# Where 1/sum is applied in windowed attention: on the weights per unit, or on the output per pair

## The chip, the cores and the metric

The kernel runs on one core of a Trainium2 chip. The metric is device time in microseconds, the median of several executions. A core has TensorE (matmuls, and the transpositions that are matmuls with an identity), VectorE, ScalarE, GpSimd, each with one in-order queue of instructions, and SyncE (SP), which issues DMAs. In profiles they are PE (PEld for its weight loads), DVE, ACT, POOL and SP.

## The reference

Attention with a sliding window of 128 and a few sink keys, followed by a dense two-layer block; batch 4, 8 heads, 768 positions, 64 per head, 512 to 2048 to 512 in the dense block:

```python
scores = scale * np.matmul(q, k.transpose(0, 1, 3, 2))
keep = is_sink | in_window
scores = np.where(keep, scores, -1000000000.0)
scores = scores - np.max(scores, axis=-1, keepdims=True)
a = np.exp(scores)
a = a / (np.sum(a, axis=-1, keepdims=True) + 1e-09)
x = np.matmul(a, v)                  # (B, H, S, D), then to (B*S, H*D)
h = x @ w_in
r = np.maximum(h, 0.0)
out = (s * (r * r) + b) @ w_out
```

## The kernel before, in words

**Chunks.** The 3072 rows are worked on in eight chunks of 384 (`ORDER`: batch and half of the sequence). While the dense block of chunk c runs (`moe_steps`: 16 steps `l1`, 16 steps `l2`, the latter two `f` behind), the attention of chunk c + 1 is issued between its steps. The main loop at L775 deals out the attention's slots evenly over the steps, over all but the last two of them. The first two chunks, both with keys of the first half only, use `Plain`, which normalises on VectorE (L523); the change does not touch it. Chunks three to eight use `attn_slots` (L413).

**Numbers as two parts.** A matmul operand in `F32R` holds only part of a float32. Where precision matters a value is split in a high part (a cast on ScalarE) and the rest (a subtraction), and the product is made from several matmuls: 12 of 384 columns per `l1` (L602), 9 of 512 per `l2` (L621).

**Units.** In `attn_slots` a chunk has 24 units: 8 heads times 3 blocks of 128 queries, two heads to a pair, two pairs to a quad. One slot issues the parts of several units:

- `unit_a` (slot t, unit t): the scores of 128 queries against two key blocks of 128 and 8 sink keys (L303, L304), on VectorE mask and minimum (L308), on ScalarE the exponential with its sum (L314). The mask leaves two triangles that don't overlap, so GpSimd adds the two 128-column squares into one (L317); the first unit of a batch has one square only. GpSimd copies the 8 sink exponentials, three times over, into `psk`, a tile per quad (L318).
- `turn` (slot t, unit t - 3): TensorE transposes the added square (L324) into a corner of the bank in which the next unit's scores are made.
- `unit_b` (unit t - 4): VectorE parts the triangles again (L337), ScalarE and GpSimd make the high and low parts `hl` (L339, L340). For the last unit of a pair it also makes 1/sum of the pair's six sums on VectorE (L349 to L353), in two parts, and puts them into columns 96 and up of `psk` (L352 on GpSimd).
- `unit_c` (unit t - 7): the products with the values (L369, L377), at the end of a head the copy to `pp.x` (L384, L385), at the end of a quad three transpositions of `psk` (L392) into `xs`.
- `sinks` (L397) then adds the sinks' product to a pair's `pp.x`, and `scaled` (L404) multiplies `xs` with `sel`, a constant of ones and zeros that gives each column's 1/sum to all rows of a head, multiplies `pp.x` by that on VectorE (L409), and splits the result in the two parts of the dense block's input `k.x` (L410, L411). `LD` and `LDL` give the slots of these two.

`sm`, the unit's exponentials, has four buffers (`SMB`). All short-lived PSUM tiles (`sc`, `o`, `h`, `ts`, `os`, `zb`) share the five banks of `psA`.

**Order.** The source order is a priority. A planner places each engine's instructions by its own model of times, among those that are ready the earliest in the source first; so instructions of neighbouring slots and steps stand mixed. What results is a fixed order per engine; on the chip each waits on semaphores for its inputs and for its buffer.

## Time and profile before

| | |
|---|---|
| median of 3 runs | 734.43 us (733.99 to 736.96) |
| profiled execution | 733.62 us, of which the span of its instructions is 731.8 us |
| TensorE matmuls busy | 697.6 us, 95% of the span |
| VectorE, ScalarE, GpSimd busy | 514.5 us (70%), 473.4 us (65%), 390.7 us (53%) |
| mean granted clock of TensorE | 0.977 |

The dense block of the first chunk starts at about 45 us and settles at about 133, until when weights are loaded and prepared. The windowed attention runs from about 150 to 655 us, beside the dense block of chunks two to seven; the last chunk's dense block has nothing beside it. Busy times of matmuls overlap, so that the time one takes is read from the start of the next. Idle time of an engine is shown with what ended it.

### The profile page before, as it was taken

Reading aid. Unit: us, or ns where it says so; the run is one execution under the profiler, and the core shown is the slowest. Engines: PE = TensorE matmul, PEld = TensorE weight load, DVE = VectorE, ACT = ScalarE, POOL = GpSimd, SP = SyncE. Lnnn points to the kernel's source line nnn. Section 1 sums busy time; section 2 is a strip of 40 time slices with the busy share of each in tenths; the row PEclk is TensorE's granted clock in tenths of the full one; section 3 lists DMA queues with packets and bytes.
Section 4 is the critical chain, followed back from the end, with each engine's and each line's share of the span. In section 5 each row is a group of like instructions: output and inputs, shape, how many; then the busy total and the mean of one; then the engine's idle time right before and its main releaser. Section 6 shows DMA issues by size and latency. Waiting matters only on the chain.

```text
span 731.8 us, 11834 instructions
## 1 busy us (share of the span) xinstructions
PE 697.6 (95%) x3812; PEld 614.7 (84%) x3812; DVE 514.5 (70%) x1202; ACT 473.4 (65%) x1157; POOL 390.7 (53%) x640
## 2 busy tenths in 40 slices
PE   6788889899999999999999999999999999999996
PEld 3367667789988999899998999899999999989895
DVE  6779999748985688757786588847786579743331
ACT  5978887558774687657784677747775577633222
POOL 2254555348983588816674388915765389810000
PEclk8889989999999999999999999999999999999999
DMA  7845122041310221111111222112111212000001
GB/s 277 344 172 194 34 91 83 12 142 42 95 57 16 94 59 55 43 62 53 45 51 56 73 68 66 45 42 61 56 52 56 72 42 63 8 15 30 0 1 47
DMA packets 27221, 52.62 MB, mean 72 GB/s; under 512 B 3472, under 2 KB 15376, under 8 KB 25232
## 3 DMA queue, kind: packets, MB, share of 16 engines
q1 hardware_dynamic: 27152, 51.79, 21.3%
q8 instruction: 32, 0.52, 0.3%
q14 instruction: 37, 0.30, 0.1%
HBM read 45.49 MB, written 6.29 MB: 71 GB/s over the span
## 4 chain that ended last, share of the span: by engine, by line
PE 76%; DVE 11%; POOL 4%; DMA 3%; ACT 3%; issue 2%; SPq 1%; POOLq 0%; ACTq 0%; DVEq 0%
PE po L621 32%; PE h L602 31%; PE o L377 3%; PE sc L303 2%; PE sc L304 2%; PE sc L324 2%; DMA vf<-in_v 2%; DVE w L214 2%; DMA w<-in_w 2%; DVE g L610 1%; DVE wt L213 1%; POOL w L216 1%; PE o L555 1%; DVE smf L532 1%; DVE w L225 1%
## 5 line engine op out<-in xcount | busy, mean ns | idle before, releaser
L602 PE MATMUL h<-x,w 128*128 128x384 f32 x1536 | 297.1, 342 | 3.2 <-DVE y L409 2.0
L621 PE MATMUL po<-w,g 128*128 128x512 f32 x1152 | 297.5, 404 | 0.0
L602 PEld LDWEIGHTS h<-x,w 128*128 128x128 f32 x1536 | 266.5, 189 | 9.7 <-DVE y L409 2.5
L621 PEld LDWEIGHTS po<-w,g 128*128 128x128 f32 x1152 | 211.0, 190 | 45.3 <-issue 2.7
L607 DVE SCALAR_TENSOR_TENSOR r<-h,sb,r 128x384 f32<-128x384 f32 x128 | 78.7, 615 | 83.1 <-ACT r L605 82.2
L610 DVE SCALAR_TENSOR_TENSOR g<-r,sb,g 128x384 fp32r<-128x384 f32 x128 | 109.1, 852 | 34.9 <-ACT g L609 33.3
L605 ACT ACTIVATE r<-h 128x384 f32<-128x384 f32 x128 | 62.4, 488 | 89.2 <-PE h L602 80.8
L340 POOL TENSOR_TENSOR hl<-two,hl 128x256 fp32r<-128x256 f32 x128 | 102.2, 800 | 15.1 <-ACT hl L339 12.9
L609 ACT ACTIVATE g<-r,sb 128x384 fp32r<-128x384 f32 x128 | 78.9, 617 | 33.1 <-DVE r L607 32.2
L317 POOL TENSOR_TENSOR sm<-sm 128x128 f32<-128x128 f32 x128 | 67.4, 527 | 60.1 <-ACT sm L314 56.7
L314 ACT ACTIVATE sm<-sm,negm 128x264 f32<-128x264 f32 (+1 forms) x144 | 72.0, 500 | 28.6 <-DVE negm L308 27.1
L284 POOL TENSOR_TENSOR kl<-kraw,kh 128x528 fp32r<-128x528 f32 (+1 forms) x48 | 60.4, 1258 | 25.9 <-ACT kh L282 25.7
L339 ACT CAST hl<-two 128x256 fp32r<-128x256 f32 x128 | 50.4, 394 | 25.8 <-DVE two L337 25.7
L216 POOL TENSOR_TENSOR w<-w 128x1024 int32<-128x1024 int32 (+1 forms) x17 | 32.6, 1918 | 55.2 <-DVE w L214 34.7
L337 DVE TENSOR_TENSOR two<-sc,split 128x256 f32<-128x256 f32 x128 | 53.1, 417 | 5.8 <-POOL hl L340 5.5
L377 PE MATMUL o<-hl,vv 128*128 128x256 f32 (+1 forms) x256 | 44.3, 275 | 0.0
L318 POOL COPY psk<-sm 128x24 f32<-128x24 f32 x144 | 35.0, 243 | 17.2 <-ACT sm L314 17.0
L283 DVE TENSOR_TENSOR qs<-qraw,qs 64x384 fp32r<-64x384 f32 x48 | 39.7, 827 | 3.8 <-ACT qs L279 2.3
L377 PEld LDWEIGHTS o<-hl,vv 128*128 128x128 f32 x256 | 39.6, 188 | 3.2
L308 DVE CUSTOM_DVE_ANT_0 sm<-sc,msk 128x264 f32<-128x264 f32 (+1 forms) x80 | 32.0, 399 | 14.1 <-PE sc L304 13.5
L303 PE MATMUL sc<-kh,qs 128*128 128x264 f32 (+1 forms) x144 | 41.6, 291 | 0.0
L308 DVE CUSTOM_DVE_ANT_0 sm<-sc,m_all 128x264 f32<-128x264 f32 x64 | 27.3, 426 | 20.3 <-PE sc L304 18.8
(129 smaller groups left out, 916.5 us busy)
## 6 DMA issues: line engine op xcount, KB each, us to landing
w<-in_w SPq DMA_DIRECT2D x15, 1024.0 KB, 9.8
kraw<-in_kT SPq DMA_DIRECT2D x32, 264.0 KB, 2.6
out<-ot SPq DMA_DIRECT2D x24, 256.0 KB, 2.0
qraw<-in_qT SPq DMA_DIRECT2D x24, 192.0 KB, 2.4
vraw<-in_v SPq DMA_DIRECT2D x16, 256.0 KB, 2.7
kraw<-in_kT SPq DMA_DIRECT2D x16, 200.0 KB, 2.4
vsraw<-in_vsk SPq DMA_DIRECT2D x24, 64.0 KB, 2.0
vraw<-in_v SPq DMA_DIRECT2D x8, 192.0 KB, 2.4
```

What stands on the lines that cost most here:

```text
L284: nc.gpsimd.tensor_tensor(out=hd.kl[:, :kw], in0=hd.k[:, :kw], in1=hd.kh[:, :kw].bitcast(F32), op=ALU.subtract)
L308: nc.vector.tensor_tensor_reduce(out=sm[:, :n], in0=sc[:, :n], in1=m, scale=-0.125, scalar=BIG, op0=ALU.add, op1=ALU.min, accum_out=negm[: ...
L314: nc.scalar.activation(sm[:, :n], sm[:, :n], AF.Exp, bias=negm[:, uu], scale=-1.0, accum_out=pp.zz[:, i, hh:hh + 1])
L317: nc.gpsimd.tensor_tensor(out=sm[:, c1:c1 + P], in0=sm[:, p1:p1 + P], in1=sm[:, c1:c1 + P], op=ALU.add)
L340: nc.gpsimd.tensor_tensor(out=lo, in0=both, in1=hi.bitcast(F32), op=ALU.subtract)
L377: nc.tensor.matmul(hd.o[:, q0:q0 + n * P], hd.vv[:, kb, :], hd.hl[:, t, c0 * P:(c0 + n) * P], start=(hd.n == 0), stop=(i == BLK - 1 and kb ...
L602: nc.tensor.matmul(h[:, :CH], weight[f][:, 0, wi, cc * P:(cc + 1) * P], x[xi][:, cc, :], start=(i == 0), stop=(i == 11))
L605: nc.scalar.activation(r, h[:, :CH], AF.Relu, scale=1.0 / WUP)
L607: nc.vector.scalar_tensor_tensor(out=r, in0=h[:, :CH], scalar=sw_ap, in1=r, op0=ALU.mult, op1=ALU.mult)
L609: nc.scalar.activation(gg[:, 0, :], r, AF.Identity, bias=b_ap, scale=1.0)
L610: nc.vector.scalar_tensor_tensor(out=gg[:, 1, :], in0=r, scalar=b_ap, in1=gg[:, 0, :].bitcast(F32), op0=ALU.add, op1=ALU.subtract)
L621: nc.tensor.matmul(po[tb], gg[:, gi, tsl], weight[f][:, 1, wi, :], start=(f == 0 and i == 0), stop=(f == NF - 1 and i == 2))
```

## The change

From the third chunk on (all of `attn_slots`), 1/sum is applied to the weights before the transposition. A new function `norm` runs in every even slot for the two units before: on VectorE it adds 1e-9 to the two sums and takes the reciprocals, on ScalarE it multiplies each unit's added square by its 1/sum, and on GpSimd the sinks' exponentials are multiplied by it on the way into `psk`, in place of the copy. `sel`, the 1/sum columns in `psk`, `scaled` and its product go; `sinks` ends a pair. The slots of `sinks` change (`LD`, `LDL`), and a chunk has 32 slots in place of 33.

```diff
--- before.py
+++ after.py
@@ -34,7 +34,7 @@
 RB, VB = 1, 2
 E0 = 8
 FN, FB, FC = (4, 2), (6, 6), (9, 10)
-LB, LC, LD, LDL, L2 = 4, 7, ((3, 4), (6, 7)), ((2, 2), (3, 3)), 2
+LB, LC, LD, LDL, L2 = 4, 7, (3, 5), (2, 2), 2
 
 
 @with_exitstack
@@ -85,8 +85,6 @@
 
 
 
-    sel = const.tile([P, 2, P], F32R, tag="sel", name="sel")
-
     psks = [const.tile([P, BLK, P], F32, tag=f"psk{i}", name=f"psk{i}") for i in range(2)]
 
     lim = const.tile([P, 2, 2], I32, tag="lim", name="lim")
@@ -132,13 +130,6 @@
 
     def constants2():
 
-        spread = wk.tile([P, 2, P], F32, tag="y", name="spread", bufs=3)
-        nc.gpsimd.memset(spread, 0.0)
-        for j in range(4):
-            row = spread[96:P, j // 2].rearrange("p (a d) -> p a d", a=2)
-            nc.gpsimd.affine_select(out=row, in_=row, pattern=[[1, 2], [0, D]], compare_op=ALU.not_equal, fill=1.0,
-                                    base=2 * j, channel_multiplier=-1)
-        nc.scalar.copy(sel, spread)
         for t in psks:
             nc.gpsimd.memset(t, 0.0)
 
@@ -252,7 +243,7 @@
             hd.q, hd.v = pp.q[hd.half], pp.v[:, :, hh]
             k.heads[2 * pr + hh] = hd
         pp.psk = psks[(k.c * (H // 4) + pr // 2) % 2]
-        pp.zz = wk.tile([P, BLK, 2], F32, tag="zz", name="zz", bufs=2)
+        pp.z = wk.tile([P, 3, 2 * BLK], F32, tag="zz", name="zz", bufs=2)
 
     def load_keys(k, h):
 
@@ -309,14 +300,26 @@
                                        op0=ALU.add, op1=ALU.min, accum_out=negm[:, uu])
 
         k.cc[(h, i)] = (sm,) + ((NS, None, 0) if g == 0 else (P, 0, 2 * P) if g % 2 else (P + NS, 0, P))
-        s0 = k.cc[(h, i)][3]
-        hh = h % 2
-        nc.scalar.activation(sm[:, :n], sm[:, :n], AF.Exp, bias=negm[:, uu], scale=-1.0, accum_out=pp.zz[:, i, hh:hh + 1])
+        nc.scalar.activation(sm[:, :n], sm[:, :n], AF.Exp, bias=negm[:, uu], scale=-1.0,
+                             accum_out=pp.z[:, 0, h % 2 * BLK + i:h % 2 * BLK + i + 1])
         if g > 0:
             c1, p1 = k.cc[(h, i)][1:3]
             nc.gpsimd.tensor_tensor(out=sm[:, c1:c1 + P], in0=sm[:, p1:p1 + P], in1=sm[:, c1:c1 + P], op=ALU.add)
-        nc.gpsimd.tensor_copy(out=pp.psk[:, i, :12 * NS].rearrange("p (t x) -> p t x", t=3)[:, :, h % 4 * NS:(h % 4 + 1) * NS],
-                              in_=sm[:, s0:s0 + NS].unsqueeze(1).to_broadcast([P, 3, NS]))
+
+    def norm(k, *two):
+
+        z = k.pairs[two[0][0] // 2].z
+        j0 = two[0][0] % 2 * BLK + two[0][1]
+        jj = slice(j0, j0 + 2)
+        nc.vector.tensor_scalar(out=z[:, 1, jj], in0=z[:, 0, jj], scalar1=1e-9, scalar2=None, op0=ALU.add)
+        nc.vector.reciprocal(out=z[:, 2, jj], in_=z[:, 1, jj])
+        for j, (h, i) in enumerate(two):
+            pp = k.pairs[h // 2]
+            sm, c0, _, s0 = k.cc[(h, i)]
+            rz = z[:, 2, j0 + j:j0 + j + 1]
+            nc.scalar.mul(sm[:, c0:c0 + P], sm[:, c0:c0 + P], rz)
+            nc.gpsimd.tensor_scalar(out=pp.psk[:, i, :12 * NS].rearrange("p (t x) -> p t x", t=3)[:, :, h % 4 * NS:(h % 4 + 1) * NS],
+                                    in0=sm[:, s0:s0 + NS].unsqueeze(1).to_broadcast([P, 3, NS]), scalar1=rz, scalar2=None, op0=ALU.mult)
 
     def turn(k, h, i, tp):
 
@@ -341,16 +344,6 @@
         else:
             nc.scalar.copy(hi, tp)
             nc.vector.tensor_tensor(out=lo, in0=tp, in1=hi.bitcast(F32), op=ALU.subtract)
-        pp = k.pairs[h // 2]
-        if h % 2 == 1 and i == BLK - 1:
-            z0 = 12 * NS + h // 2 % 2 * 4
-            zr = wk.tile([P, 2, BLK, 2], F32, tag="zr", name="zr")
-            zh = wk.tile([P, BLK, 2], F32R, tag="zh", name="zh")
-            nc.vector.tensor_scalar(out=zr[:, 0], in0=pp.zz, scalar1=1e-9, scalar2=None, op0=ALU.add)
-            nc.vector.reciprocal(out=zr[:, 1], in_=zr[:, 0])
-            nc.vector.tensor_copy(zh, zr[:, 1])
-            nc.gpsimd.tensor_copy(out=pp.psk[:, :, z0:z0 + 2], in_=zh.bitcast(F32))
-            nc.vector.tensor_tensor(out=pp.psk[:, :, z0 + 2:z0 + 4], in0=zr[:, 1], in1=zh.bitcast(F32), op=ALU.subtract)
 
     def unit_c(k, h, i):
 
@@ -400,13 +393,6 @@
         os_ = ps("os")
         nc.tensor.matmul(os_[:, :CH], pp.vs, pp.xs, start=True, stop=True)
         nc.vector.tensor_tensor(out=pp.x, in0=os_[:, :CH], in1=pp.x, op=ALU.add)
-
-    def scaled(k, pr):
-
-        pp = k.pairs[pr]
-        zb = ps("zb")
-        nc.tensor.matmul(zb[:, :CH], sel[:, pr % 2], pp.xs, start=True, stop=True)
-        nc.vector.tensor_tensor(out=pp.x, in0=zb[:, :CH], in1=pp.x, op=ALU.mult)
         nc.scalar.copy(k.x[0][:, pr, :], pp.x)
         (nc.vector if pr == H // 2 - 1 else nc.gpsimd).tensor_tensor(out=k.x[1][:, pr, :], in0=pp.x, in1=k.x[0][:, pr, :].bitcast(F32), op=ALU.subtract)
 
@@ -424,8 +410,7 @@
         ends = {}
         for pr in range(H // 2):
             t = 4 * BLK * (pr // 2 + 1) - 1 + LC
-            for d, fn in zip((LD if pr < H // 2 - 2 else LDL)[pr % 2], (sinks, scaled)):
-                ends.setdefault(t + d, []).append((fn, pr))
+            ends.setdefault(t + (LD if pr < H // 2 - 2 else LDL)[pr % 2], []).append((sinks, pr))
 
         def slot(t):
             def f():
@@ -440,6 +425,8 @@
                     unit_a(k, *units[t], k.bank)
                 if 0 <= t - LB < n:
                     unit_b(k, *units[t - LB], k.bank[:, 3 * P:])
+                if t % 2 == 0 and 0 < t <= n:
+                    norm(k, *units[t - 2:t])
                 for fn, pr in ends.get(t, ()):
                     fn(k, pr)
                 if t + 1 < n + LB:
@@ -448,7 +435,7 @@
                     turn(k, *units[t + 1 - LB], k.bank[:, 3 * P:])
             return f
 
-        parts = [slot(t) for t in range(n + LC + LDL[1][1])]
+        parts = [slot(t) for t in range(n + LC + LDL[1])]
         parts.pop(n + LB)
         return k, parts
 
```

## Rows read from the trace of the kernel before

**Rows 1.** Stretches: us, busy PE, PEld, DVE, ACT, POOL, clock, DMA share, GB/s

```profile
323.00:405.00 82.00, 82.00 (x463) 75.26 (x462) 59.57 (x147) 54.78 (x149) 47.15 (x87) 1.00 0.18 57
405.00:491.00 86.00, 85.53 (x483) 78.29 (x482) 62.68 (x147) 58.52 (x150) 58.15 (x103) 1.00 0.18 56
```

**Rows 2.** Chain of waits, 431 to 448 us: start, length in us, what

```profile
433.32 0.41 PE o L377 x4
...
434.86 2.10 PE po L621 x9
...
440.24 2.10 PE po L621 x9
...
445.47 2.10 PE po L621 x9
```

**Rows 3.** By line and shape: count | busy us, mean ns | idle before

```profile
L602 PE MATMUL h<-x,w 128*128 128x384 f32 x1536 | 297.1, 342 | 3.2 <-DVE y L409 2.0 <-ACT tf L546 1.2
...
L409 DVE TENSOR_TENSOR y<-zb,y 128x384 f32<-128x384 f32 x24 | 13.2, 552 | 0.7
...
L350 DVE RECIPROCAL zr<-zr 128x6 f32<-128x6 f32 x24 | 4.6, 191 | 0.8
...
L351 DVE CAST zh<-zr 128x6 fp32r<-128x6 f32 x24 | 7.7, 322 | 0.5
...
L353 DVE TENSOR_TENSOR psk<-zr,zh 128x6 f32<-128x6 f32 x24 | 7.2, 302 | 0.7
...
L521 ACT ACTIVATE smf<-smf,negm 128x128 f32<-128x128 f32 x8 | 3.1, 389 | 1.9 <-DVE negm L519 1.9
...
L270 ACT CAST vs<-vsraw 128x128 fp32r<-128x128 f32 x24 | 6.6, 295 | 0.8 <-DMA vsraw<-in_vsk 0.8
...
L532 DVE TENSOR_SCALAR sm<-sm,zf 128x128 f32<-128x128 f32 x8 | 1.9, 284 | 0.1
...
L610 DVE SCALAR_TENSOR_TENSOR g<-r,sb,g 128x384 fp32r<-128x384 f32 x128 | 109.1, 852 | 34.9 <-ACT g L609 33.3
...
L609 ACT ACTIVATE g<-r,sb 128x384 fp32r<-128x384 f32 x128 | 78.9, 617 | 33.1 <-DVE r L607 32.2
```

**Rows 4.** List of waits, whole execution: us in total, times, longest us

```profile
PE h L602 <- DVE y L409: 2.0, 3, 1.1
```

**Rows 5.** In order of time, TensorE, 401 us: start, length in us, what

```profile
401.19 0.34 PE L408 MATMUL zb<-xsk,sel 128*128 128x384 f32 x1
401.36 0.40 PE L621 MATMUL po<-w,g 128*128 128x512 f32 x1
```

**Rows 6.** In order of time, 303 to 305 us: VectorE, TensorE

```profile
303.64 0.56 DVE L409 TENSOR_TENSOR y<-zb,y 128x384 f32<-128x384 f32 x1
...
304.26 0.97 PE L602 MATMUL h<-x,w 128*128 128x384 f32 x4 [0.43 <-DVE y L409]
```

**Rows 7.** In order of time, GpSimd, first 8 us

```profile
7.37 0.52 POOL L159 COPY msk<-m_all 128x128 bf16<-128x128 bf16 x2 [3.27 <-DVE m_all L101]
```

**Rows 8.** L349 and L318 alone: ns shortest/median/longest, first and last start

```profile
L349 DVE TENSOR_SCALAR zr<-zz x24: 207/322/803, 167.5 to 633.2; 128x6 f32<-128x6 f32 x24
...
L318 POOL COPY psk<-sm x144: 193/203/546, 156.7 to 634.0; 128x24 f32<-128x24 f32 x144
```

**Rows 9.** In order of time: L314's read, then L324, three pairs

```profile
157.33 0.19 ACT L314 ACTIVATION_READ_ACCUMULATOR sm<-sm,negm 128x1 f32 x1
159.06 0.27 PE L324 MATMUL sc<-identr,sm 128*128 128x128 f32 x1
...
520.97 0.18 ACT L314 ACTIVATION_READ_ACCUMULATOR sm<-sm,negm 128x1 f32 x1
521.66 0.27 PE L324 MATMUL sc<-identr,sm 128*128 128x128 f32 x1
...
632.97 0.19 ACT L314 ACTIVATION_READ_ACCUMULATOR sm<-sm,negm 128x1 f32 x1
635.98 0.27 PE L324 MATMUL sc<-identr,sm 128*128 128x128 f32 x1
```

## The prediction

> **What bounds the kernel now.** I read the busy time by stage first. From 323 to 405 us TensorE's matmuls are busy for 82.00 of 82.00 us, from 405 to 491 for 85.53 of 86, both at a granted clock of 1.00, the 2.4 GHz level [rows 1]. VectorE stands at 59.6 and 62.7, ScalarE at 54.8 and 58.5, GpSimd at 47.2 and 58.2 in the same stretches [rows 1]. A busy TensorE row alone is weak evidence, as matmuls overlap; so I read the chain of waits over 15 us of one chunk [rows 2]: it steps from matmul group to matmul group, with no other engine between. In the six chunks with the windowed attention the time is therefore the sum of what TensorE is given, plus what it waits. Third, the groups by line tell where it waits: before L602 it sat idle 3.2 us in the whole execution, and 2.0 of them ended with VectorE's L409, a line that the change deletes [rows 3]; the list of waits has three of these, the longest of 1.1 us [rows 4]. Fourth, the instructions in order of time around one use of the deleted product and around one of the waits [rows 5, 6].
>
> **What is removed, on the path.** (a) The product with `sel`, L408: 24 matmuls, one per pair of heads and chunk. The price is the step from its start to the next matmul's, 401.19 to 401.36, 0.17 us [rows 5]; its listed time, 0.34, overlaps the next one and is the upper bound. 24 x 0.17 = 4.1 us, at most 8.2. I take 4.1, as the step is what the next matmul really waited; TensorE has no idle time there to hide it. (b) The three waits on L409, 2.0 us [rows 4]. The one at 304.26 shows the kind [rows 6]: `h` starts 0.06 us after VectorE's product ends. `h` needs a PSUM bank, `zb` still holds it, and VectorE is late with L409. The four small instructions of L349, L350, L351 and L353 are gone after (0.32 + 0.19 + 0.32 + 0.30 = 1.1 us [rows 3, 8]), and so is L409 (0.55), 1.7 us of queue against waits of at most 1.1; and `zb` claims no bank. I take 2.0; the bounds are 0 (another bank is as late) and 2.0.
>
> **What is removed, beside the path.** VectorE loses per pair those five instructions, 24 x 1.7 = 41 us. GpSimd loses L352, a copy of 6 columns. Neither shortens anything by itself. The making of `sel` (a memset, four selects, a copy) lies ahead of a stretch of 3.27 us in which GpSimd stands idle, until 7.37 us [rows 7]: nothing. The end of a pair moves: `sinks` takes over the cast and the subtraction of L410 and L411, as many as before, and for a chunk's second pair it comes a slot earlier; no DMA is added or moved, and no queue of SP or GpSimd gets another one.
>
> **What is added.** (c) 144 multiplies of 128x128 on ScalarE (`nc.scalar.mul` with a scalar per partition). The trace has no such instruction. The nearest is L521's 128x128 activation, also from SBUF to SBUF with an operand per partition: 389 ns; below it lies the plain 128x128 cast of L270, 295 ns, above it L609's 128x384, 617 [rows 3]. I take 0.39: 24 x 0.39 = 9.4 us per chunk, and ScalarE goes from 58.5 to 68 of 86 us [rows 1]. It keeps 18 us idle per chunk (13 at 617), so its load costs nothing; only its order can. (d) 72 additions and 72 reciprocals of 128x2 on VectorE, like L349 and L350: 72 x (0.32 + 0.19) = 37 us, against the 41 that go [rows 3, 8]: VectorE is no busier. (e) On GpSimd 144 copies of 24 columns become multiplies with a scalar per partition. Bounds: 193 and 546 ns, the shortest and the longest copy; I take 0.25, a little over the median of 203, as the size is the copy's [rows 8]. At 546 it is 24 x 0.34 = 8.2 us more per chunk, 66 of 86: still idle time. What reads it, the transposes of `psk`, comes six slots later.
>
> **The new wait, and who stands behind it.** Until now a unit's transposition (L324) waited for the exponential and GpSimd's addition. Now it waits for the reciprocals of a pair of units, made in the slot after the second, and then for ScalarE. So I measured the room: from the end of the second unit's sum (the accumulator read of L314) to the start of the first unit's L324. In 72 pairs it runs from 0.5 to 3.9 us, median 2.9: first pair 157.52 to 159.06, 1.54; last 633.16 to 635.98, 2.82; the shortest 521.15 to 521.66, 0.5 [rows 9]. Into that room go 0.21 (the shortest L349) + 0.19 + 0.39 = 0.79 us of work, about 0.9 with the hand-overs. Two pairs have less room; at a lag of 1.2 us six are short, by 2.1 us in sum (each pair's lag less its room, added up). The short ones are units 10 and 11 of a chunk, where two slots (11 and 12) fall between two steps of the dense layers; with 32 slots in place of 33 over 30 steps there is one such place left after the first step (16 and 17), not two (11 and 12, 22 and 23). I take half of 2.1, **1.0 us**. Bounds: 0, as the planner may put other matmuls ahead of a late transposition, and the rivals below.
> Behind the waiting multiply on ScalarE stand the casts of `hl` (L339) and the dense layers' L605 and L609. What these make is needed late: an `h` that is done at 433.32 is used by the third `po` group after, at 445.47 [rows 2], 12 us for four instructions of which the longest takes 0.85 [rows 3]. Behind GpSimd's waiting multiply stand L317 and L340, whose result is used three slots later. Behind VectorE's addition stands L308, which is followed by the exponential and gives a bank free: the sharpest of these.
>
> **Where a page and the trace meet.** L349, the addition's model, took 207, 322 and 803 ns at its shortest, median and longest, with the same 6 columns [rows 8]. The Trainium skill (GPSIMD Engine Reference, Specifications) says that GpSimd shares its SBUF interface with VectorE and that they contend when VectorE runs in a two-port mode or reads two SBUF inputs; by that rule the long ones met a GpSimd instruction. With the long value throughout, the lag is 0.80 + 0.19 + 0.39 = 1.4 us, and the waits, by the room of the same pairs, some 3.5 us in place of 1.0.
>
> **The sum.** -4.1 - 2.0 + 1.0 = -5.1 us. The profiled execution took 733.62 us (731.8 its span, 1.8 around it), so 728.5; the median of before, 734.43, is 0.8 above it, so the forecast for the median is **729.3**. With (b) at 0 and at 2.0 and the new waits at 2.1 and at 0 it lies between 732.4 and 728.3.
>
> **Rivals.** *One: the bank stays late.* `h` waits for the bank of `os` or of a transposition instead, since VectorE is late there for another reason too, L337's wait for GpSimd. Only (a) is gained: 734.43 - 4.1 + 1.0 = 731.3. Against it: 1.7 us of VectorE's queue goes.
> *Two: the waits move to L324.* If the lag is 1.8 us, one instruction in the way on ScalarE or VectorE each time, nine pairs are short by 6.6 us in sum: 734.43 - 6.1 + 6.6 = 734.9. For it: ScalarE prepares the next head at the short pairs. Against: TensorE's idle time is so small today that the planned order suits the real durations.
> *Three: slower.* ScalarE's queue sets the pace at L324. With one long instruction ahead on VectorE (L610, 0.85) and one on ScalarE (L609, 0.62) the lag is 0.79 + 0.85 + 0.62 + 0.1 = 2.4 us [rows 3]; 23 of the 72 pairs are short, by 16.1 us in sum: 734.43 - 6.1 + 16.1 = 744.4. It makes the kernel slower by over half a per cent from a lag of about 2.0 us on (9.3 us in sum, against 6.1 gained). For it: 9.4 us more per chunk in one in-order queue. Against: most pairs have over 2.4 us, and another matmul can go first. The Trainium skill (ScalarE: Activation LUTs, Rules for kernel authors) sends multiplications to VectorE rather than ScalarE; by that rule this rival gains. The trace prices 128x128 at 284 ns on VectorE (L532) against 389 [rows 3], and VectorE is the busier of the two [rows 1].
>
> **Chances.** A measurement of this kernel can tell about 0.5% (3.7 us) from no change: 730.8 and 738.1 are the borders. Forecast 0.55 (0.50 of it under 730.8), one 0.15 (a third of it under), two 0.18, three 0.12. Faster 0.55, same 0.33, slower 0.12. The range runs from 726.0 to 736.5: below, 728.3 less 0.4 for the spread of the runs and 1.9 for a step of 0.25 us, not 0.17, per product, between the bounds of (a); above, rival two and 1.6 more, a lag of 1.9 us. Rival three is left out.
>
> **What would show it.** Right: no L408; each stretch of rows 1 shorter by 0.7 us (four products), and three of the six chunks by their wait as well; no idle time before L602 that ends with a VectorE instruction on a bank; ScalarE at about 68 of 86, with one multiply of 0.39 us per unit. Wrong: idle time of TensorE before L324 that ends with ScalarE's multiply (rivals two and three, by its sum), or before L602 with L402 or L337 (rival one). What would upset the whole: a multiply that takes far over 0.6 us, or a new order of the first 150 us, which I took as untouched.

## The result, and the profile after

The changed kernel takes 741.12 us (median of 14 executions, 734.06 to 744.08); the kernel before, beside it, 734.42 (14 executions). The ratio is 1.0076, interval 1.0052 to 1.0099: by that ratio slower by 5.6 us (the medians differ by 6.7), where 5.1 less was forecast. The profiled execution took 741.20 us, against 733.62.

I cut an execution in three: the *start*, up to the first `h` matmul of chunk two's dense block; the *middle*, from there to the first one of the last chunk, in which the windowed attention runs beside six dense blocks; and the rest. TensorE in order of time, after (start and length in us), with the first `h` of all ahead:

```profile
51.77 3.18 PE L589 MATMUL h<-x,w 128*128 128x384 f32 x10
...
157.22 2.28 PE L589 MATMUL h<-x,w 128*128 128x384 f32 x12
...
664.91 6.52 PE L589 MATMUL h<-x,w 128*128 128x384 f32 x36
```

The same three of before:

```profile
44.92 2.65 PE L602 MATMUL h<-x,w 128*128 128x384 f32 x10
...
151.75 2.27 PE L602 MATMUL h<-x,w 128*128 128x384 f32 x12
...
657.68 6.52 PE L602 MATMUL h<-x,w 128*128 128x384 f32 x36
```

| us | before | after | difference |
|---|---|---|---|
| start | 151.75 | 157.22 | +5.5 |
| middle | 505.94 | 507.69 | +1.8 |
| rest | 74.1 | 74.5 | +0.4 |

Starts and middles are taken from the trace in ns, so one can differ by 0.01 from the rows. There are two questions: why the first 150 us, in which no instruction was added, got longer, and why the middle, from which 24 products and three waits went, did not get shorter.

**The middle.** The stretches of [rows 1], after (us; PE, PEld, DVE, ACT, POOL, clock, DMA share, GB/s):

```profile
323.00:405.00 82.00, 80.50 (x453) 73.63 (x452) 54.73 (x150) 62.04 (x172) 50.51 (x83) 1.00 0.18 54
405.00:491.00 86.00, 84.55 (x478) 77.31 (x477) 63.28 (x152) 65.06 (x174) 62.69 (x100) 1.00 0.19 57
```

TensorE, which had no gap in the first and 0.47 us in the second, now has gaps of 1.5 us in each. ScalarE rose by 7.3 and 6.5 us, GpSimd by 3.4 and 4.5; VectorE's 59.6 fell to 54.7, and its 62.7 became 63.3. Groups by line and shape, answering [rows 3] (idle before, with what ended it):

```profile
L589 PE MATMUL h<-x,w 128*128 128x384 f32 x1536 | 299.2, 343 | 3.1 <-DVE hl L346 2.4 <-ACT tf L533 0.7
...
L320 ACT ACTIVATE sm<-sm,zz 128x128 f32<-128x128 f32 x144 | 51.7, 395 | 5.5 <-DVE zz L315 5.0
...
L327 PE MATMUL sc<-identr,sm 128*128 128x128 f32 x144 | 39.9, 277 | 2.4 <-ACT sm L320 1.7 <-DVE two L340 0.5
```

List of waits in the place of [rows 4], 150 to 665 us (total us, times, longest):

```profile
PEld o L362 <- POOL hl L343: 3.9, 4, 1.0
...
PEld sc L327 <- ACT sm L320: 3.0, 4, 1.1
PEld h L589 <- DVE hl L346: 2.8, 2, 1.4
```

The three waits on the old product are gone, and three other kinds are there, 9.7 us in sum by the weight loads (PEld): on GpSimd's low part of the attention weights, on ScalarE's new multiply, and on VectorE's low part of a batch's first unit. Only the second waits for the multiply itself. What lies behind the third is shown by the chain of waits (start, length, what), where [rows 2] went from matmul to matmul:

```profile
384.22 0.32 ACT x L396
...
384.64 0.41 ACT sm L320
...
385.06 0.49 ACT r L592
385.56 0.29 ACT sm L320
385.84 0.49 ACT sm L303 x2
386.34 0.53 ACT g L596
...
386.89 0.19 DVE g L597
...
387.45 0.29 DVE hl L346
...
387.79 2.35 PE h L589 x12
```

For 2.6 us the chain does not leave ScalarE: seven instructions stand back to back, two of them the new multiplies, on an engine that is busy for 62 of 82 us in this stretch. The two multiplies take 0.7 us of these 2.6. The dense block's `r` and `g` stand behind them, so VectorE comes late to L346, the `h` matmuls get their bank late, and TensorE stands for 1.2 us. Nothing in that chain waits for 1/sum.

The small operations, answering [rows 8] (ns shortest/median/longest):

```profile
L314 DVE TENSOR_SCALAR zz<-zz x72: 150/178/681, 163.1 to 642.8; 128x2 f32<-128x2 f32 x72
...
L321 POOL TENSOR_SCALAR psk<-sm,zz x144: 334/345/752, 163.5 to 646.2; 128x24 f32<-128x24 f32 x144
```

**The start.** From 15 to 30 us, before, then after (columns as above):

```profile
15.00:30.00 15.00, 13.09 (x82) 8.54 (x83) 11.46 (x54) 13.91 (x29) 1.89 (x1) 0.87 1.01 415
```

```profile
15.00:30.00 15.00, 14.13 (x56) 7.62 (x58) 7.80 (x31) 9.92 (x22) 0.00 (x0) 0.56 1.01 416
```

56 matmuls are done in place of 82, at a mean granted clock of 0.56 in place of 0.87 (most of the stretch at 1.2 GHz), and ScalarE, VectorE and GpSimd are behind as well. The first `h` comes 6.9 us later, as the first rows above show. The executions of the changed kernel lie in two groups: six from 734.06 to 736.46 at mean clocks of 0.980 to 0.985, eight from 741.05 to 744.08 at 0.965 to 0.973, and the profiled one is of the second.

### The profile page after: what moved, and what is told of

Same layout as the page of the kernel before. It is cut to its first block, busy times and chain, and to the rows that moved or that the text cites. A ratio compares the mean times of both kernels' runs of the same rounds, so it can differ in the third digit from the quotient of the medians.

```text
span 739.4 us, 11938 instructions
## 1 busy us (share of the span) xinstructions
PE 699.2 (95%) x3788; PEld 614.0 (83%) x3788; DVE 507.4 (69%) x1226; ACT 516.1 (70%) x1300; POOL 413.8 (56%) x611
## 4 chain that ended last, share of the span: by engine, by line
PE 65%; DVE 16%; ACT 11%; issue 3%; POOL 2%; DMA 2%; SPq 0%; ACTq 0%; DVEq 0%; POOLq 0%
PE h L589 27%; PE po L608 25%; DVE g L597 3%; PE o L370 2%; DVE w L205 2%; ACT sm L303 2%; DVE qs L274 2%; PE sc L294 2%; ACT sm L320 2%; PE sc L295 1%; PE sc L327 1%; DVE wt L204 1%; DVE r L594 1%; PE tp L531 1%; PE o L542 1%
## 5 line engine op out<-in xcount | busy, mean ns | idle before, releaser
L608 PE MATMUL po<-w,g 128*128 128x512 f32 x1152 | 296.3, 402 | 0.0
L608 PEld LDWEIGHTS po<-w,g 128*128 128x128 f32 x1152 | 210.5, 190 | 42.9 <-issue 2.8
L597 DVE SCALAR_TENSOR_TENSOR g<-r,sb,g 128x384 fp32r<-128x384 f32 x128 | 99.1, 774 | 41.8 <-ACT g L596 40.4
L343 POOL TENSOR_TENSOR hl<-two,hl 128x256 fp32r<-128x256 f32 x128 | 99.9, 783 | 7.8 <-ACT hl L342 7.6
L307 POOL TENSOR_TENSOR sm<-sm 128x128 f32<-128x128 f32 x128 | 69.3, 541 | 56.6 <-ACT sm L303 50.5
L275 POOL TENSOR_TENSOR kl<-kraw,kh 128x528 fp32r<-128x528 f32 (+1 forms) x48 | 61.6, 1283 | 32.4 <-ACT kh L273 32.1
L321 POOL TENSOR_SCALAR psk<-sm,zz 128x24 f32<-128x24 f32 x144 | 58.7, 422 | 9.9 <-DVE zz L315 8.8
L320 ACT ACTIVATE sm<-sm,zz 128x128 f32<-128x128 f32 x144 | 51.7, 395 | 5.5 <-DVE zz L315 5.0
L274 DVE TENSOR_TENSOR qs<-qraw,qs 64x384 fp32r<-64x384 f32 x48 | 46.8, 975 | 8.8 <-ACT qs L270 7.7
L280 POOL TENSOR_TENSOR vv<-vraw,vv 128x256 fp32r<-128x256 f32 (+1 forms) x48 | 33.2, 692 | 31.7 <-ACT vv L279 31.2
L327 PE MATMUL sc<-identr,sm 128*128 128x128 f32 x144 | 39.9, 277 | 2.4 <-ACT sm L320 1.7
```

What stands on the lines that cost most here:

```text
L275: nc.gpsimd.tensor_tensor(out=hd.kl[:, :kw], in0=hd.k[:, :kw], in1=hd.kh[:, :kw].bitcast(F32), op=ALU.subtract)
L307: nc.gpsimd.tensor_tensor(out=sm[:, c1:c1 + P], in0=sm[:, p1:p1 + P], in1=sm[:, c1:c1 + P], op=ALU.add)
L320: nc.scalar.mul(sm[:, c0:c0 + P], sm[:, c0:c0 + P], rz)
L343: nc.gpsimd.tensor_tensor(out=lo, in0=both, in1=hi.bitcast(F32), op=ALU.subtract)
L597: nc.vector.scalar_tensor_tensor(out=gg[:, 1, :], in0=r, scalar=b_ap, in1=gg[:, 0, :].bitcast(F32), op0=ALU.add, op1=ALU.subtract)
L608: nc.tensor.matmul(po[tb], gg[:, gi, tsl], weight[f][:, 1, wi, :], start=(f == 0 and i == 0), stop=(f == NF - 1 and i == 2))
```

## The experiments: the start

**e1 and e2: the making of `sel`, and nothing else.** e1 is the changed kernel with `sel` made as before, though nobody reads it. e2 is the kernel before with `sel` made later, behind the weights of the first chunk.

```diff
 # e1: after
+    sel = const.tile([P, 2, P], F32R, tag="sel", name="sel")
     def constants2():
+        spread = wk.tile(...)   # memset, four selects, nc.scalar.copy(sel, spread)
 # e2: before: the same lines moved from constants2() to
+    make_sel()                  # behind first_cm, ahead of the main loop
```

> The changed kernel with one thing put back: the constant sel is made at the start as before (one memset, four selects, one copy), though nothing reads it. The planned order of every engine is then that of the kernel before up to the first windowed unit. Theory 1 (the loss is made in the first 150 us, by another planned order and the lower clock that goes with it; the middle costs 1.8 us): the dense block of the second chunk starts at about 152 us, not 157, and the median is 734.4 + 1.8 = 736, ratio about 1.002. Rival (the loss is that of the new waits in the middle, the start differs by chance): 740 to 741, ratio 1.007.

> The kernel before with one thing changed: sel is made late, by about 50 us, so that the planned order of the first 50 us is that of the changed kernel; all of the windowed attention is as before. Theory 1: the start of the second chunk's dense block goes from 152 to about 157 us in many executions, the times spread as those of the changed kernel do, median 738 to 740, ratio 1.005 or more. Rival: 734.4, ratio 1.000 with the start at 152.

e1: 733.72 us (12 executions, 732.49 to 738.72), ratio 1.0007 (0.9982 to 1.0033); start 149.94, middle 507.59. e2: 739.95 (7 executions, 732.58 to 741.53), ratio 1.0063 (1.0034 to 1.0093), though its profiled execution is its fastest, with a start of 149.93 and a middle of 506.83. The middle of e1 is that of the changed kernel, so all of the difference between the two is in the start. Moving one constant, which nobody reads in that time, makes the kernel before slower by 4.6 us by the ratio (6.1 by the medians); keeping it, useless, takes the loss from the changed kernel. GpSimd had time for it, as the prediction said. But the planner's order of the first 50 us hangs on it: with it ScalarE's copy of `sel` is the second instruction in the engine's trace, without it an exponential is, and from there on the orders of TensorE, VectorE, ScalarE and GpSimd differ. In the traces e1 has the order of before on all four engines up to the first windowed unit (about 156 us), and e2's TensorE has the order of the changed kernel for its first 170 matmuls, up to 47 us.

**e15 and e16: is it the clock?** 40 matmuls on a tile of zeros, whose result nobody reads, are offered to TensorE behind the attention of the first chunk, and land in its empty places of the first 40 us.

```diff
+    keep_warm(40)    # nc.tensor.matmul(wp, warm[:, :P], warm, start=True, stop=True), 40 times
     first_cm.__exit__(None, None, None)
```

> The changed kernel with 40 matmuls on a tile of zeros offered to TensorE from the first instruction on, whose result nobody reads: they lie in its empty places of the first 40 us. If the long start of the changed kernel (157.2 us to the first h matmul of chunk two in its profiled execution, with TensorE at 1.2 GHz from 16.8 to 30.5 us) is the lower clock after an idle stretch, the time at 1.2 GHz falls below 10 us there, the start is 150 to 153 us in every execution, and the time 733 to 736 us. If the longer start is the planned order itself, it stays at 155 to 158 us in more than half of the executions and the median near 740 us.

> The kernel before with the same 40 matmuls. By the clock theory its start (151.75 us, 6.8 us at 1.2 GHz between 12.2 and 19.0) shortens by at most half of those 6.8 us: 731 to 734 us, and its executions lie closer together. By the theory of the order nothing falls, and the added matmuls cost 0 to 3 us where they stand ahead of work that is ready: 734 to 737 us.

e15, the changed kernel: 746.65 us (6 executions, 744.78 to 749.46), ratio 1.0168 (1.0132 to 1.0204); e16, the kernel before: 744.27 (6, 743.33 to 744.83), ratio 1.0125 (1.0094 to 1.0157). Both theories missed: neither foresaw that the start grows by 5.6 and by 10.9 us. The stretch of e15:

```profile
15.00:30.00 15.00, 14.15 (x84) 7.74 (x84) 11.59 (x53) 11.65 (x29) 1.89 (x1) 1.00 1.01 417
```

The clock is now at its full 2.4 GHz there, 84 matmuls are done in place of 56 (some of the added ones among them), and yet the start is 162.85 us. So the empty places were not free: 10.2 us of added matmuls within the first 50 us (52 on the zeros in place of 14) went with starts that are longer by 5.6 and 10.9 us. And they are no test of the clock. They raised it in this stretch, but over the first 150 us its mean is 0.89 in e15 against 0.88 in the changed kernel, and 0.90 in e16 and in before alike; in e15 it is 0.77 from 45 to 60 us and 0.83 from 120 to 150. The planned order of the real work changed too, so the clock's share is not isolated. One thing can be read: with the added matmuls the two starts are the same (162.85 and 162.61), and what is left between the kernels, 2.4 us by the medians, is mostly the middle (507.45 and 505.81).

**Is it the order?** Not alone. e2's profiled execution has the changed kernel's order of TensorE up to 47 us, and this stretch:

```profile
15.00:30.00 15.00, 11.73 (x69) 7.32 (x69) 10.73 (x43) 11.74 (x27) 1.89 (x1) 0.88 1.01 415
```

In one and the same order 69 matmuls are done here in place of 56, at 0.88 in place of 0.56, and the start is 149.93 in place of 157.22. The other way about, e6 (below), which keeps e1's order of the start, had a start of 156.97 us, at 0.969 over the whole execution, where e1 had 149.94. So either order can have the short start and the long one. How often is told by the times: 8 of the changed kernel's 14 executions are above 741 us, and 5 of e2's 7 above 737.8, while the slowest of the 80 executions of the kernel before that ran beside the experiments took 737.76. Across these 80, of one order, the time goes mostly with the mean clock: 732.8 to 733.5 at 0.979 to 0.981, 735.1 to 737.1 at 0.973 (and one of 732.93 at 0.960). At 0.980 to 0.981 the changed kernel takes 734.1 to 735.7, some 2 us more, which is the middle. At 0.973 it takes 741.1 to 741.2, 4 us or more above before, and e2 took 739.95 at 0.976, where before took 733.4 to 734.7; so the mean clock does not give the time by itself. The new order has the long times more often: that much is shown. How it brings the long stretch at 1.2 GHz about, and whether that stretch is the cause of the time or goes along with it, stays open.

## The experiments: the middle

All of these are edits of e1 (its order of the start, its line numbers), except e4, which is one of before. A middle is read from one execution, the profiled one. It repeats: e14 and e17, which are the same kernel, have 503.36 and 503.53, and e1 and e6, in one order of TensorE, 507.59 and 507.45. e5, e6, e9, e12 and e13 ran once, so that for them only the middle is compared. e3, e5, e6, e9 and e13 leave out the division or a part of it.

**e3, e5, e6: what is gained, and what each added part costs.** e3 leaves out the whole division by the sums, e5 the division of the squares, e6 that of the sinks.

```diff
 # e3: no add, reciprocal, multiply; GpSimd copies as before
-            nc.scalar.mul(sm[:, c0:c0 + P], sm[:, c0:c0 + P], rz)
-            nc.gpsimd.tensor_scalar(... scalar1=rz, op0=ALU.mult)
+            nc.gpsimd.tensor_copy(...)
 # e5: only the first of these lines goes;  e6: only GpSimd's multiply becomes the copy
```

> As e1, and nothing is divided by the sums: no addition, no reciprocal, no multiply on ScalarE, and GpSimd copies the sinks' exponentials as before. It prices what the change removes. Prediction's terms (a) and (b): 4.1 us for 24 products and 2.0 (2.5 by the steps between matmuls) for the three waits, so the middle, from the second chunk's dense block to the last one's, goes from 505.9 to about 499.5, the time to about 728. Rival one (the bank stays late): only 4.1, middle 501.8, time 730.3.

> As e1 (sel kept for the order of the start), without the multiply of the added square on ScalarE: the squares stay undivided, the sinks are divided. The middle is 507.6 us in e1 and 496.2 without any norm (e3): 11.4 us of new waits. Theory 2a (ScalarE's multiply makes most of them): the middle falls to 497 to 500. Theory 2b (GpSimd's multiply, 345 ns by the median where the copy took 203, or the pair's reciprocals): it stays at 504 to 507.

> As e1, with GpSimd's multiply turned back into the copy: the sinks stay undivided, the squares are divided on ScalarE. Theory 2a: the middle stays at 505 to 507, the waits of TensorE that end with GpSimd's low parts (3.6 us in e1) among them. Theory 2b: it falls to 498 to 501, these 3.6 us first.

e3: 723.38 us (4 executions), ratio 0.9862 (0.9825 to 0.9899), middle 496.19. e5: 723.5 (one execution), middle 496.02. e6: 740.65 (one), of it a start of 156.97 us, and a middle of 507.45. Stretches of e5:

```profile
323.00:405.00 82.00, 82.00 (x465) 75.65 (x464) 57.24 (x154) 56.75 (x151) 51.69 (x86) 1.00 0.20 57
405.00:491.00 86.00, 86.00 (x491) 79.52 (x491) 63.75 (x156) 60.33 (x156) 64.38 (x103) 1.00 0.20 57
```

So the removal is worth 505.94 - 496.02 = 9.9 us of the middle (the terms (a) and (b) had led to 499.5 in e3, not 496.2), and the multiply of the squares costs 507.59 - 496.02 = 11.6, all that was gained and 1.7 more. The additions, the reciprocals and GpSimd's multiplies cost nothing: e5 still has them, and TensorE has no gap; e6 is e1 within 0.15 us.

**e4: the multiply alone, in the kernel before.** 144 multiplies by one, directly behind GpSimd's addition.

```diff
             nc.gpsimd.tensor_tensor(out=sm[:, c1:c1 + P], ..., op=ALU.add)
+        nc.scalar.mul(sm[:, c1:c1 + P], sm[:, c1:c1 + P], one)   # c1 of either kind of unit
```

> The kernel before with 144 multiplies of the added squares by one, on ScalarE, ahead of the transposition; the product with sel stays, TensorE's planned order is the same as before. It prices ScalarE's multiply alone. Theory 2a (ScalarE's queue makes the new waits): the middle rises from 505.9 by 3 us or more, with waits of TensorE that end with ScalarE's multiply or with GpSimd's low parts. Theory 2b (the pair's reciprocals or GpSimd's slower multiply make them): it rises by less than 1 us.

758.52 us (4 executions), ratio 1.0327 (1.0288 to 1.0367); the middle 530.25, 24.3 us longer, though TensorE's instructions stand in the same order as before. The list of waits:

```profile
DVE r L608 <- ACT r L606: 116.3, 87, 4.5
...
ACT sm L318 <- POOL sm L317: 40.0, 75, 1.1
```

ScalarE waits for GpSimd's sum in 75 of 144 places, up to 1.1 us, and its whole queue with it. So this is the same work in a worse place, and no price for the change; it shows how much the place can cost. Its expectation (3 us or more) was met in size, but TensorE's waits end mostly with VectorE's L608, behind ScalarE, and none with the multiply itself.

**e9 and e13: the link of the chain, the place, or the load.** e9 writes the product into the dead `sel`: ScalarE does all it did, but the transposition no longer waits for it, and the squares stay undivided. e13 does the same on 8 columns in place of 128. In e5, e9 and e13 TensorE's instructions stand in one and the same order.

```diff
-            nc.scalar.mul(sm[:, c0:c0 + P], sm[:, c0:c0 + P], rz)
+            nc.scalar.mul(sel.bitcast(F32)[:, j], sm[:, c0:c0 + P], rz)            # e9
+            nc.scalar.mul(sel.bitcast(F32)[:, j, :8], sm[:, c0:c0 + 8], rz)        # e13
```

> As e1, but ScalarE's multiply writes into a tile that nothing reads (the unused sel), so that the transposition takes the undivided square: the same 144 multiplies with the same inputs in the same place of the source, and no wait of the transposition for them. Without the multiply the middle was 496.0 us (e5), with it 507.6 (e1). Theory 3a (the multiply costs as a link of the chain from the scores to the transposition): 496 to 499. Theory 3b (it costs as work in ScalarE's in-order queue): 503 to 508. In between: both.

> e9 with its 144 ScalarE multiplies cut from 128 columns to 8; their result is read by nobody and the squares stay undivided. Number, place and waits of the instructions are e9's, only their length falls. If the 9.3 us of the middle that e9 had over e5 (505.3 against 496.0) are the length of the multiplies on ScalarE, the middle falls in the measure in which an instruction gets shorter: to 498 to 500 us if 8 columns take a third of 0.39 us or less. If they are the place in the queue, where ScalarE holds what stands behind while the multiply waits for the pair's sum, the middle stays at 504 to 506 us.

e9: 731.79 us (one execution), middle 505.33. e13: 728.15 (one), middle 500.43. The multiply in e9 and in e13:

```profile
L329 ACT ACTIVATE sel<-sm,zz x144: 385/394/404, 157.0 to 636.2; 128x128 f32<-128x128 f32 x144
```

```profile
L329 ACT ACTIVATE sel<-sm,zz x144: 283/296/303, 158.1 to 632.6; 128x8 f32<-128x8 f32 x144
```

Of the 11.6 us, 505.33 - 496.02 = 9.3 are paid with nobody waiting for the result; the link of the chain is worth 507.59 - 505.33 = 2.3, as against 1.7 (groups) to 3.0 (list) that TensorE waits for L320; some of TensorE's order differs between these two as well. In e13 98 ns less per multiply, 14 us of ScalarE's time in all, give back 4.9 of the 9.3, in the same place behind the same waits. That is the load, and it is steep: a quarter of the multiply's length costs half of the 9.3. The remaining 4.4 us belong to the 43 us of work that are left and to its place, which e13 does not part.

**e7, e8, e14, e17, e18: on which engine.** e7: the squares' multiply on VectorE; e8: the sinks' on VectorE; e14: the even unit's square on ScalarE and the odd one's on VectorE, with `norm` in the place of e12 (below); e17: by its text e14 with the place of e12, but e14 has that place already, so it is the same kernel again; e18: that kernel with the engines exchanged.

```diff
+            if j == 0:          # e18: j == 1;  e7: no if
                 nc.scalar.mul(sm[:, c0:c0 + P], sm[:, c0:c0 + P], rz)
+            else:
+                nc.vector.tensor_scalar(out=sm[:, c0:c0 + P], in0=sm[:, c0:c0 + P], scalar1=rz, scalar2=None, op0=ALU.mult)
 # e14, e17, e18: and norm(...) ahead of unit_a(...), as in e12
 # e8
-            nc.gpsimd.tensor_scalar(out=pp.psk...
+            nc.vector.tensor_scalar(out=pp.psk...
```

> As e1, with the added squares multiplied on VectorE, not ScalarE; all of the computation is there. VectorE has 284 ns for such a square in the rows of before, ScalarE 393 in the changed kernel; VectorE stands at about 63 of 86 us, ScalarE at 64.5. Theory 2a (ScalarE's in-order queue: its casts for the next head come late behind the multiplies, and then VectorE's and GpSimd's subtractions fall together): the middle falls by 3 us or more, to 504 or less. Rival (the work has no better place, a multiply on VectorE delays the release of banks): 508 or more, TensorE's waits ending with VectorE.

> As e1, with the sinks' multiply on VectorE, not GpSimd; all of the computation is there. It takes 144 times 0.35 to 0.42 us from GpSimd and gives VectorE 144 short ones. Theory 2b (GpSimd): the waits that end with GpSimd's low parts, 3.6 us, go and the middle is 504 or less. Theory 2a: 506 to 509.

> e1 with the multiply of the even unit of each pair on ScalarE and that of the odd one on VectorE; what is computed is the reference's. If the price is one of load on a single queue, half of it on each engine costs less than all on either: middle 499 to 504 us against 507.6 (all on ScalarE) and 508.1 (all on VectorE), and the time 726 to 731 us. If the price is the same on both because each multiply stands in the pair's chain and both queues feed TensorE, the middle stays at 505 to 508 us and the time at 731 to 735 us.

> e14 and e12 together: even unit's multiply on ScalarE, odd unit's on VectorE, and the pair's sums, reciprocal and multiplies ahead of the next unit's products in the program. If the two savings of the middle (e14 4.2, e12 2.3 of e1's 507.6) come from different waits they add: middle 501 to 502 us, time 729 to 731 us, faster than the kernel before by 0.4 to 0.7%. If both relieve the same spot of ScalarE's queue, the middle stays at 503 us and the time at 731 to 732 us.

> e17 with the engines exchanged: odd unit's multiply on ScalarE, even unit's on VectorE; work and load of each engine are e17's. By the load alone its middle is e17's within 0.5 us. By the place in the queue it differs by 1 to 2 us either way, since ScalarE's multiply then stands behind the second reciprocal of the pair and ahead of the next unit's exponential.

| | us, executions | ratio to before | middle |
|---|---|---|---|
| e1, all on ScalarE | 733.72, 12 | 1.0007 (0.9982 to 1.0033) | 507.59 |
| e7, all on VectorE | 736.01, 10 | 1.0027 (1.0001 to 1.0054) | 508.10 |
| e8, sinks on VectorE too | 741.3, 6 | 1.0105 (1.0072 to 1.0139) | 513.39 |
| e12, all on ScalarE, e12's place | 734.03, 1 | | 505.34 |
| e14, half and half, e12's place | 731.76, 10 | 0.9974 (0.9945 to 1.0002) | 503.36 |
| e17, the same kernel | 731.55, 12 | 0.9983 (0.9960 to 1.0006) | 503.53 |
| e18, halves exchanged | 732.63, 12 | 0.9989 (0.9970 to 1.0008) | 504.22 |

In e1's place the same 144 multiplies cost 11.6 us on ScalarE and 12.1 on VectorE. In e12's place they cost 9.3 on ScalarE and 7.3 to 7.5 when each engine has half (8.2 in e18). So of the 4.2 us between e1 and e14 the place has 2.3 and the halving 1.8 to 2.0; e12 and e14 have one and the same order of TensorE. Two stretches of e14, in the place of [rows 1]:

```profile
323.00:405.00 82.00, 81.73 (x458) 74.68 (x457) 59.87 (x163) 59.39 (x161) 50.88 (x83) 1.00 0.19 56
405.00:491.00 86.00, 85.34 (x482) 78.30 (x482) 64.02 (x163) 61.99 (x162) 62.46 (x99) 1.00 0.20 61
```

VectorE and ScalarE stand at 64.0 and 62.0 of 86 us, and TensorE's gaps shrink to 0.3 and 0.7. What the halving takes away is most of the wait before `h` that ends with the low part of a batch's first unit, the one behind ScalarE's seven instructions in the chain above; 150 to 665 us, e12, then e14:

```profile
PEld h L598 <- DVE hl L355: 2.8, 2, 1.4
```

```profile
PEld h L601 <- DVE hl L358: 0.6, 2, 0.3
```

That speaks for the load in a single queue, not for one engine's being unfit. Whether the savings of the place and of the halving add was not tested: no run has the halves in e1's place. e18 lies 0.7 us above e17, between its two theories. e8 missed both of its own (506 to 509, or 504 and less): on VectorE the sinks' multiply costs 5.8 us more than on GpSimd, in the same order of TensorE. With the whole computation e14 (twice) and e18 are the fastest, 1.2 to 2.4 us under the kernel before by the medians; each interval reaches 1, so none is shown to beat it.

**e10, e11, e12: when.** e10 makes `norm` per unit, a slot earlier for the first of a pair; e11 lets `unit_c` come a slot later; e12 calls `norm` ahead of `unit_a` in its slot.

```diff
-                if t % 2 == 0 and 0 < t <= n:                          # e10
-                    norm(k, *units[t - 2:t])
+                if 0 < t <= n:
+                    norm(k, *units[t - 1:t])
-LB, LC, LD, LDL, L2 = 4, 7, (3, 5), (2, 2), 2                          # e11
+LB, LC, LD, LDL, L2 = 4, 8, (2, 4), (1, 1), 2                          # and no slot dropped: 33
```

> As e1, with the norm made for each unit in the slot after it, not for two units in every second slot: the first of two units has its reciprocal a slot (2.7 us) earlier, VectorE has 144 more instructions of 0.17 us. All of the computation is there. Theory 3a: the middle falls from 507.6 to 503 or less. Theory 3b: it stays or rises, 507 to 510.

> As e1, with the products with the values one slot later (LC 8, the sinks at the same slots, 33 slots): GpSimd's low parts have 2.7 us more until TensorE needs them. All of the computation is there. If the waits for the low parts (3.6 us in e1) are lateness handed down from the multiply, they go: middle 504 or less. If a later use only keeps buffers longer (hl has two): 508 or more.

> As e1, with the norm ahead of the slot's scores in the source, so that the planner prefers it to the new unit's mask and exponential. All of the computation is there. Theory 3a: the multiplies end earlier, middle below 506. Theory 3b: about 507 to 509, as ScalarE's work is the same.

e10: 752.47 us (4 executions), ratio 1.0264 (1.0233 to 1.0296), middle 523.77. e11: 744.65 (4), ratio 1.0167 (1.0121 to 1.0213), middle 516.25. e12: 734.03 (one), middle 505.34. More room for the multiply or for `hl` did not help, and e10's price was far over both of its theories (up to 510). In e10 each unit has a wait of its own: ScalarE's multiply waits 28 times for the reciprocal and 30 times for GpSimd's sum, 35 us in all; in e11, which relieves the wait for GpSimd's `hl` (none is left of its 3.9 us), the wait for the multiply grows from 3.0 to

```profile
PEld sc L336 <- ACT sm L329: 12.1, 12, 1.3
```

Only the place in the program, ahead of the next unit's work, gives something back (2.3 us).

## Why the prediction was wrong

**(c), ScalarE's multiplies, "its load costs nothing": this step failed.** The duration was right (0.39 us forecast, median 0.393), and ScalarE's share came out below the forecast (65.06 of 86, not 68, since its instructions overlap their neighbours by about 0.1 us). The inference was wrong: 18 us of idle time per chunk were no cover in an in-order queue whose work comes in bunches, as in the chain above. 9.3 us of the middle are paid with nobody waiting for the product (e9 against e5), and 4.9 of them for a quarter of its length (e13). The prediction named the casts of `hl` and the dense layers behind the multiply, and took them as needed late (12 us of room for an `h`); the chain at 384 to 388 us shows the way it missed, from a late `r` and `g` to VectorE, and from there to a bank of PSUM. Why the load is so steep, and what part of the price is the place in the queue, stays open.

**The new wait, 1.0 us with bounds of 0 and 2.1:** 1.7 to 3.0 at the transposition by the rows, 2.3 by e9 against e1: around its upper bound, mis-sized by a factor of some 2. What it left out is that most of the price would fall elsewhere.

**(a) + (b), 6.1 us:** 9.9 by e5. The products' steps in the middle sum to 4.2, as forecast; the steps that begin with a transposition, the 2.0 us of gaps before `h` among them, are shorter by 3.5; the rest, 2.2, is spread over slightly shorter steps of `po`, `sc` and `o`. The order of TensorE differs between the two, and this rest has no cause that is shown. So the sum that was forecast as -4.1 - 2.0 + 1.0 = -5.1 is -9.9 + 11.6 = +1.7 in the middle.

**The making of `sel`, "nothing", and the first 150 us, "untouched":** 5.5 us in the profiled execution, and by e1 nearly all of the loss (the ratio falls from 1.0076 to 1.0007). The prediction named this as what would upset it, but priced the work and not its part in the order.

**(d) and (e)** held: VectorE is not busier, GpSimd's multiply took 345 ns by the median, over the 250 taken and inside the bounds, and costs nothing (e6).

**The rivals.** Rival three had the right cause, ScalarE's in-order queue, but its price was put at L324 alone, from a lag of 2.0 us on; it was paid at `h`, `o` and their banks. The sentence on the Trainium skill there (ScalarE: Activation LUTs, Rules for kernel authors: multiplications to VectorE) would have made e7 the better version; e7 is not (508.10 against 507.59), though one multiply took 335 ns there by the median against 393. Rival one came true in kind: `h` waits 2.4 us for the bank of a transposition, released by VectorE's L346, about as long as it had waited for L409 (2.0). But VectorE was late there behind ScalarE's queue, not behind L337's wait for GpSimd, and without the multiply (e5) the wait is gone. Rival two did not happen: the waits at L327 are too small.

The fault common to both failed steps: each took spare time of an engine, a mean over a stretch, for freedom to put work there.

## What to carry to other kernels

Where one engine is full and a second, in-order one feeds it at 70% busy, price added work on the second by trying it, or by the bunches in its queue, not by its mean idle time. Here half of it on another engine's queue gave back 1.8 to 2.0 of 9.3 us, and an earlier place in the program 2.3. Where a planner orders the queues, an instruction that is removed or moved far from the critical path is a change of the whole order around it: keep a dead copy of it once, to see which part of the difference is the order.

## What the hardware showed beside that

In the changed kernel a VectorE instruction as small as 128x2 (L314, an addition of a constant) took 150 to 681 ns. What decides is whether a GpSimd instruction is already running when it starts. In 28 of the 72 places none was, and it took 151 to 171 ns, also where one started beside it. In the other 44 one was; in 40 of these L314 ended 21 to 30 ns after that one's end, whichever it was (L262, L275, L280, L307 or L343), and in the other four GpSimd was done at least 44 ns before L314's end. Two of them, with two different GpSimd instructions:

```profile
304.95 1.05 POOL L275 TENSOR_TENSOR kl<-kraw,kh 128x400 fp32r<-128x400 f32 x1
...
305.36 0.67 DVE L314 TENSOR_SCALAR zz<-zz 128x2 f32<-128x2 f32 x1
...
607.16 0.74 POOL L343 TENSOR_TENSOR hl<-two,hl 128x256 fp32r<-128x256 f32 x1 [0.53 <-ACT hl L342]
607.24 0.68 DVE L314 TENSOR_SCALAR zz<-zz 128x2 f32<-128x2 f32 x1
```

L315, the reciprocal of the same two columns, was never held: 148 to 168 ns, though in 57 of 72 places GpSimd was running at its start, as here:

```profile
200.64 0.46 POOL L307 TENSOR_TENSOR sm<-sm 128x128 f32<-128x128 f32 x1
...
200.74 0.17 DVE L315 RECIPROCAL zz<-zz 128x2 f32<-128x2 f32 x1
```

The Trainium skill (GPSIMD Engine Reference, Specifications) says that GpSimd shares its SBUF interfaces with VectorE, and that they contend when VectorE's instruction runs in a two-port mode or reads two SBUF inputs. The trace agrees in that one kind of VectorE instruction is held and another is not; in which mode either ran, no run here shows. In the kernel before, all 24 of L349 started beside a running GpSimd instruction and ended 26 to 34 ns after it, the one of 207 ns too; so the prediction's median of 322 ns for that addition was in good part a wait.

On ScalarE 8 columns took 296 ns and 128 took 394, 0.8 ns per column: some three quarters of the longer one's time do not depend on its length.
